# Taking 110 products of zeros out of the front of a gated-recurrence and gated-MLP kernel

## The chip, the cores and the metric

The kernel runs on one core of a Trainium2 chip. The metric is the time of one execution on the device in microseconds (us), measured from outside; the profile of one execution shows the span from that execution's first instruction to its last. TensorE (PE in the rows) multiplies, its weight loads are shown apart (PEld); VectorE (DVE), ScalarE (ACT) and GpSimd (POOL) do the rest, and SyncE (SP) issues nearly all DMA transfers.

## What is computed

For 4 batches and 8 heads, a recurrence over 768 tokens with a 48x48 state and a gate for each row, and then a gated MLP with a mixing matrix over the tokens:

```python
f = 1.0 / (1.0 + np.exp(-f_logit))
for t in range(S):
    state = f[:, :, t, :, None] * state + np.einsum('bhd,bhe->bhde', k[:, :, t], v[:, :, t])
    y[:, :, t] = np.einsum('bhd,bhde->bhe', q[:, :, t], state)
# x: y with the heads side by side, (4, 768, 384)
h = np.maximum(x @ w_in, 0.0)
u, v = (h[..., :d_ff // 2], h[..., d_ff // 2:])
v_n = (v - mean(v)) / np.sqrt(var(v) + 1e-06)
v_s = np.einsum('ts,bsd->btd', w_spatial, v_n) + b_spatial[None, :, None]
return ((u * v_s) @ w_out).astype(np.float32)
```

## The kernel before

The tokens of a batch are cut into 6 blocks of 128, which makes 24 blocks, numbered n = 0 to 23. The recurrence is done block by block in chunk form. For each block: `LF`, `LK`, `LQ` load the gate logits, keys and queries, and values; `c`, `e` clip the logits and take a logarithm of the gate (ACT, lines 325 and 326); `z` sums these along the tokens, for blocks 0 to 7 by products with a triangle on TensorE (line 336); `h` and `g` are exponentials of the sums (ACT, 342 and 347); `q` and `k` scale queries and keys (DVE, 357 and 353); `X` makes the scores (PE, 381); `w` and `m` take them out of PSUM (ACT 387, DVE 391); `YS`, `kv` and `Yq` are the products with values and state (PE, 435, 405, 447); `r0`, `r1`, `r2` update the state (DVE 411/413 and 419, POOL 426); `ys`, `xt`, `xh`, `xl` take the block's output out, transpose it (PE, 459) and split it into two parts for the MLP.

The MLP works on these outputs with every operand split into a rounded part and a rest, in three passes: `V` (PE, 492), `U` (PE, 577), `S` (PE, 591) and `O` (PE, 622), with their steps on the other engines. Before `V` can run, its weights have to be loaded (`LV`, `LU`, `LO`, line 242, from the 64-bit form in which they lie in memory) and converted: `ca` (ACT, 251), `ct` (DVE, 256 to 258), `ch` (ACT, 265) and `cl` (DVE, 271). The token matrix is split by `wh` (ACT, 289) and `wl` (DVE, 293) after its loads `LW`.

The order of all steps is written out in one table, `PLAN`. A loop runs through it, and each step issues its instructions, so the table gives the order on every engine; an engine takes its own instructions strictly in that order, and waits by semaphores are put in from the data. Nothing moves a step at run time.

One kind of step, `D:n`, computes nothing that is used: n products of a tile of zeros, `junk`, with itself, into a PSUM tile `warm` that `W0` takes at the start and `W1` gives back after block 4's `r1`. They stand in the table between the steps of blocks 0 to 4:

```python
    def step_W0():
        mm.take("warm")

    def step_D(count):
        for _ in range(count):
            nc.tensor.matmul(mm.of("warm")[:, 0:2 * P], junk[:, 0:P], junk[:, 0:2 * P], start=True, stop=True)

    def step_W1():
        mm.done("warm")
```

`junk` is set to zero on DVE (line 206) ahead of everything else, and is written later by ACT (line 526), which only wants a sum and throws the elements away.

Of the kernel before, what the change touches and what calls it, by code (L numbers as in the profile page):

```python
# [41 lines left out]


PLAN = """
    LF:1 LF:0 constants W0 LF:2 LQ:1 LQ:0 c:1 e:1 LK:1 c:0 c:2 e:0 D:23 z:1 LK:0 e:2 D:1 z:0 LV:1 h:1 D:1 z:2 g:1
# [4 lines left out]
    z:4 xl:1 fm:3 ca:O,1 LQ:4 r0:2 c:5 r1:2 LW:2,0 D:1 V:0,1 ca:U,0 ct:O,1 ca:U,1 e:5 X:3 Yq:2 vr:0,1 LF:6 z:5 r2:2  # L50
    m:3 LK:6 w:3 ct:U,0 ys:2 D:1 YS:3 h:4 D:1 xt:2 g:4 kv:3 xh:2 LQ:5 wh:2,0 r0:3 c:6 r1:3 D:8 Yq:3 ch:U,0 xl:2 r2:3
    D:3 V:0,2 ys:3 k:4 h:5 q:4 g:5 cl:U,0 e:6 X:4 k:5 vr:0,2 xt:3 LK:7 z:6 m:4 fm:4 fm:5 xh:3 nm:0,0 w:4 xl:3 YS:4
    LF:7 vc:0,2 wl:2,0 D:1 U:0,0,1 sq:0,2 q:5 vc:0,0 ct:U,1 U:0,0,0 sq:0,0 vc:0,1 kv:4 sq:0,1 X:5 LQ:6 r0:4 c:7
    ur:0,0,0 r1:4 W1 Yq:4 LF:8 na:0,0 w:5 m:5 r2:4 V:0,3 nb:0,0 h:6 nc:0,0 g:6 fm:6 q:6 vh:0,2 YS:5 k:6 kv:5 ys:4
    vl:0,2 X:6 e:7 LQ:7 c:8 xt:4 LF:9 m:6 vr:0,3 z:7 r0:5 e:8 bs:0,3 Yq:5 r1:5 w:6 z:8 YS:6 h:7 kv:6 ys:5 q:7 g:7
    LQ:8 xt:5 r0:6 fm:7 vh:0,0 r1:6 Yq:6 k:7 xh:5 vl:0,0 xh:4 X:7 ch:U,1 xl:5 r2:6 LF:10 xl:4 w:7 V:0,5 cl:U,1 moe
    h:8 g:8 m:7 fm:8 vh:0,1 LB q:8 V:0,4 vr:0,5 vl:0,1 ys:6 bs:0,5 ch:O,1 xt:6 k:8 vr:0,4 YS:7 kv:7 xh:6 bs:0,4 X:8
    ur:0,0,1 LQ:9 xl:6 U:0,0,3 w:8 LF:11 cl:O,1 na:0,1 m:8 V:1,0 nb:0,1 ur:0,0,3 nc:0,1 LW:0,1 vn:0,5 U:0,0,2 vn:0,3
    vh:0,5 vn:0,4 vh:0,3 vl:0,5 vh:0,4 vl:0,3 vr:1,0 ur:0,0,2 vl:0,4 wh:0,1 bs:1,0 S:0,0,3 c:11 c:9 e:11 c:10 wl:0,1
    e:9 S:0,0,0 LO:0 r0:7 sg:0,0,3 e:10 z:9 z:10 Yq:7 YS:8 r1:7 sm:0,0,3 ys:7 sg:0,0,0 kv:8 ca:O,0 xt:7 z:11 LQ:10  # L60
    S:0,0,1 sh:0,0,3 xh:7 sl:0,0,3 xl:7 sm:0,0,0 ct:O,0 sh:0,0,0 U:0,1,0 V:1,1 ur:0,1,0 sl:0,0,0 ch:O,0 r2:7
    sg:0,0,1 cl:O,0 h:9 U:0,1,1 vr:1,1 LW:1,1 q:9 g:9 r0:8 sm:0,0,1 S:0,0,2 ur:0,1,1 r1:8 bs:1,1 r2:8 sh:0,0,1 k:9
    h:10 g:10 sl:0,0,1 fm:9 wh:1,1 Yq:8 k:10 X:9 ys:8 q:10 U:0,1,3 wl:1,1 w:9 LF:12 m:9 fm:10 xt:8 ur:0,1,3 sg:0,0,2
    X:10 LW:2,1 xh:8 sm:0,0,2 YS:9 xl:8 w:10 kv:9 LF:13 m:10 sh:0,0,2 V:1,2 sl:0,0,2 c:12 r0:9 e:12 LQ:11 r1:9
    O:0,0,0 r2:9 vr:1,2 z:12 h:11 U:1,0,2 g:11 bs:1,2 fm:11 oc:0,0,0 na:1,0 wh:2,1 od:0,0,0 c:13 O:0,0,2 k:11 nb:1,0
    wl:2,1 ur:1,0,2 e:13 nc:1,0 S:0,1,0 vn:1,0 oc:0,0,2 vn:1,2 od:0,0,2 vn:1,1 z:13 O:0,0,1 sg:0,1,0 sm:0,1,0
    S:0,1,2 oc:0,0,1 sh:0,1,0 od:0,0,1 sl:0,1,0 U:1,0,0 sg:0,1,2 S:0,1,3 ur:1,0,0 Yq:9 sg:0,1,3 YS:10 ys:9 q:11
    kv:10 xt:9 sm:0,1,3 r0:10 LQ:12 X:11 xh:9 r1:10 sh:0,1,3 Yq:10 LF:14 w:11 S:0,1,1 sl:0,1,3 ys:10 m:11 h:12 xl:9
    g:12 fm:12 q:12 k:12 xt:10 vh:1,0 sg:0,1,1 YS:11 vh:1,2 c:14 kv:11 vh:1,1 X:12 vl:1,0 LQ:13 e:14 U:0,1,2 r0:11
    sm:0,1,1 LF:15 m:12 r1:11 vl:1,2 h:13 Yq:11 w:12 z:14 V:1,3 ur:0,1,2 ys:11 q:13 g:13 vl:1,1 xh:10 xt:11 sh:0,1,1  # L70
    k:13 YS:12 vr:1,3 sl:0,1,1 kv:12 xh:11 X:13 xl:10 fm:13 LQ:14 sm:0,1,2 r0:12 U:1,0,1 w:13 LF:16 bs:1,3 sh:0,1,2
    r1:12 V:1,4 ur:1,0,1 m:13 h:14 xl:11 g:14 fm:14 c:15 V:1,5 sl:0,1,2 e:15 c:16 k:14 vr:1,4 z:15 U:1,1,0 e:16
    bs:1,4 vr:1,5 O:0,1,2 ur:1,1,0 z:16 bs:1,5 Yq:12 oc:0,1,2 YS:13 na:1,1 ys:12 od:0,1,2 kv:13 q:14 nb:1,1 O:0,1,0
    LQ:15 r0:13 nc:1,1 vn:1,4 vn:1,5 vh:1,4 xt:12 X:14 vn:1,3 oc:0,1,0 vl:1,4 xh:12 od:0,1,0 Yq:13 vh:1,3 O:0,1,1
# [36 lines left out]

# [712 lines left out]
```

## Time and profile before

| | |
|---|---|
| median of 3 runs | 361.62 us (361.6 to 361.71) |
| the profiled execution | 361.57 us, of which the span is 359.9 us |
| PE busy | 348.2 us (97% of the span), 4688 products |
| DVE busy | 217.1 us (60%) |
| ACT busy | 177.2 us (49%) |
| POOL busy | 64.1 us (18%) |
| granted TensorE clock, mean | 0.997 |

The share of a busy engine says little about what a stretch is worth; the front, up to some 50 us, has loads, weight conversions and short products that wait for each other, and behind it the long products of the MLP fill PE. In the rows an fp32 product stands as two records, so a step `X` with 16 products is a row of x32.

### The profile page before, as it was taken

The numbers are of one execution on the slowest core, as the hardware profiler recorded it, in microseconds if no ns is written. First come the engines' busy times: TensorE is split into PE (matmuls) and PEld (weight loads), VectorE is DVE, ScalarE is ACT, GpSimd is POOL, SyncE is SP. The second block draws the span as 40 slices with busy tenths as digits, with TensorE's granted clock in tenths as the row PEclk, the third lists the DMA queues.
The fourth block names the chain that finished last, engine by engine and source line by source line (L and its number), as shares of the span: only waits on it lengthen the run. The fifth ranks groups of instructions, "written<-read, shape, count | busy, mean of one in ns | idle before, by whom it ended". The sixth has DMA issues, their size and how long they took to land.

```text
span 359.9 us, 10676 instructions
## 1 busy us (share of the span) xinstructions
PE 348.2 (97%) x4688; PEld 319.2 (89%) x4688; DVE 217.1 (60%) x417; ACT 177.2 (49%) x355; POOL 64.1 (18%) x82
## 2 busy tenths in 40 slices
PE   7999999999999999999999999899999999999993
...
PEclk9999999999999999999999999999999999999998
...
GB/s 258 326 323 292 97 169 165 244 102 67 136 151 25 105 120 111 128 50 0 111 117 85 104 155 53 156 47 22 2 0 2 24 46 25 44 0 2 9 59 75
DMA packets 14983, 36.03 MB, mean 100 GB/s; under 512 B 1488, under 2 KB 10192, under 8 KB 14928
## 3 DMA queue, kind: packets, MB, share of 16 engines
...
q10 hardware_dynamic: 144, 0.20, 0.2%
...
## 4 chain that ended last, share of the span: by engine, by line
PE 84%; DVE 7%; DMA 4%; ACT 2%; issue 1%; SPq 0%; DVEq 0%; ACTq 0%
PE mm L591 27%; PE mm L622 13%; PE mm L577 13%; PE mm L492 12%; PE bp L381 5%; PE bp L447 3%; DMA late<-w_cv 3%; PE mm L672 2%; PE bp L435 2%; PE mm L459 2%; PE mm L336 2%; DMA fkq<-fkq 2%; PE bp L405 2%; DVE q L357 1%; DVE fkq L331 1%
## 5 line engine op out<-in xcount | busy, mean ns | idle before, releaser
L607 POOL TENSOR_TENSOR uT<-gt,uT 128x384 f32<-128x384 f32 x32 | 35.9, 1122 | 159.5 <-DVE gt L600 102.2
L615 DVE TENSOR_TENSOR gl<-uT,gh 128x384 fp32r<-128x384 f32 x32 | 18.6, 585 | 35.3 <-ACT gh L611 25.2
L591 PE MATMUL mm<-w_sph,vnh 128*128 128x384 f32 x192 | 39.7, 341 | 0.0
L591 PE MATMUL mm<-w_spl,vnh 128*128 128x384 f32 x192 | 39.0, 338 | 0.0
L591 PE MATMUL mm<-w_sph,vnl 128*128 128x384 f32 x192 | 39.0, 338 | 0.0
L600 DVE TENSOR_TENSOR gt<-mm,b_bc 128x384 f32<-128x384 f32 x32 | 17.8, 555 | 34.9 <-PE mm L591 34.7
L611 ACT CAST gh<-uT 128x384 fp32r<-128x384 f32 x32 | 16.4, 514 | 42.0 <-POOL uT L607 35.1
L582 ACT ACTIVATE uT<-mm 128x384 f32<-128x384 f32 x32 | 15.7, 490 | 41.1 <-PE mm L577 41.1
L591 PEld LDWEIGHTS mm<-w_sph,vnh 128*128 128x128 f32 x192 | 33.8, 188 | 0.7 <-ACT vnh L558 0.3
L591 PEld LDWEIGHTS mm<-w_spl,vnh 128*128 128x128 f32 x192 | 34.2, 188 | 0.0
L591 PEld LDWEIGHTS mm<-w_sph,vnl 128*128 128x128 f32 x192 | 34.2, 188 | 0.0
L366 POOL COPY ends<-F 112x4 f32<-112x4 f32 x24 | 10.9, 453 | 98.0 <-ACT F L342 98.0
L357 DVE TENSOR_TENSOR q<-fkq,F 112x512 f32<-112x512 f32 x24 | 19.6, 816 | 9.5 <-PE bp L447 5.4
L381 PE MATMUL bp<-q,fkq 48*64 48x112 f32 x768 | 23.6, 261 | 0.7 <-DVE q L357 0.7
L577 PE MATMUL mm<-xTh,w_inh 128*128 128x384 f32 x96 | 23.5, 353 | 0.0
L381 PEld LDWEIGHTS bp<-q,fkq 48*64 48x64 f32 x768 | 18.8, 133 | 4.0 <-issue 1.6
L512 DVE BATCH_NORM_STATS2 six<-vr 128x6 f32<-128x512 f32 x21 | 14.4, 686 | 12.9 <-ACT vr L506 12.9
L391 DVE TENSOR_TENSOR sc<-bp,mask 128x512 f32<-128x512 f32 x24 | 16.5, 689 | 9.3 <-ACT W L387 3.7
L577 PE MATMUL mm<-xTh,w_inl 128*128 128x384 f32 x96 | 22.1, 338 | 0.0
L577 PE MATMUL mm<-xTl,w_inh 128*128 128x384 f32 x96 | 22.1, 338 | 0.0
L622 PE MATMUL mm<-w_outh,gh 128*128 128x384 f32 x96 | 21.9, 344 | 0.0
L492 PE MATMUL mm<-w_inh,xTh 128*128 128x512 f32 x72 | 21.7, 409 | 0.0
...
## 6 DMA issues: line engine op xcount, KB each, us to landing
...
```

What stands on the lines that cost most here:

```text
L357: other("q", n, nc.vector).tensor_tensor(qs[n % 2][:, :, :, 0:C], *(x.rearrange("p (j c t) -> p j c t", c=T // C, t=C) for x in (parts(n)[ ...
L381: nc.tensor.matmul(sc[to, e, cs], k[dr, at:at + C], qs[n % 2][dr, j, chunk], start=True, stop=True)
L391: nc.vector.tensor_tensor(Ss[n % 2].rearrange("p (e j t) -> p e j t", e=2, t=C), scores(n)[:, :, :, 0:C], mask.unsqueeze(1).unsqueeze(1).b ...
L492: nc.tensor.matmul(acc, xs[:, c, ut * P:(ut + 1) * P], ws[:, c, G:FF], start=i == 0, stop=i == 3 * KX - 1)
L577: nc.tensor.matmul(acc[:, 0:TH], ws[:, kx, cs], xs[:, kx, :], start=i == 0, stop=i == 3 * KX - 1)
L582: nc.scalar.activation(uTs.take((b, th, c)), mm.of(("u", b, th, c))[:, 0:TH], AF.Relu)
L591: nc.tensor.matmul(acc[:, 0:TH], vns.of((b, ks))[va][:, cs], w_sp_s[wb][:, ks, th * TH:(th + 1) * TH], start=i == 0, stop=i == 3 * KS - 1,)
L600: nc.vector.tensor_tensor(gts.take((b, th, c)), mm.of(("s", b, th, c))[:, 0:TH], b_bc[:, th * TH:(th + 1) * TH], op=ALU.add)
L607: nc.gpsimd.tensor_tensor(uT, gts.of((b, th, c)), uT, op=ALU.mult)
L611: nc.scalar.copy(gs.take((b, th, c), HU)[0], uTs.of((b, th, c)))
L615: nc.vector.tensor_tensor(lo, uTs.of((b, th, c)), hi.bitcast(F32), op=ALU.subtract)
L622: nc.tensor.matmul(acc[:, 0:DM], gs.of((b, th, c))[ga][:, ts], w_out_s[wb][:, c, :], start=c == cs[0] == 0 and ga == wb == 0, stop=c == cs ...
```

## The change

Every `D` step is taken out of `PLAN`: D:23, 1, 1, 8, 4, 7, 14, 1, 5, 22, 9, 1, 1, 1, 8, 3 and 1, together 110 products and their 110 weight loads. The order of all other steps, the tiles, `W0` and `W1` (so the PSUM tile stays taken as long as before) and the setting of `junk` stay. The table is set in lines of the same width again and is one line shorter, so each line number after it is smaller by one. The first line of the table, before and after:

```diff
-    LF:1 LF:0 constants W0 LF:2 LQ:1 LQ:0 c:1 e:1 LK:1 c:0 c:2 e:0 D:23 z:1 LK:0 e:2 D:1 z:0 LV:1 h:1 D:1 z:2 g:1
+    LF:1 LF:0 constants W0 LF:2 LQ:1 LQ:0 c:1 e:1 LK:1 c:0 c:2 e:0 z:1 LK:0 e:2 z:0 LV:1 h:1 z:2 g:1 q:1 h:0 k:1
```

On PE, at the scores of the first two blocks (`X:1` writes bp_134, `X:0` writes bp_135, L381 before and L380 after), the order before is:

```order
L381 MATMUL bp_134<-q_124,fkq_113 64x112 x16
L672 LDWEIGHTS junk
L672 MATMUL mm_130<-junk 128x256
L672 LDWEIGHTS junk
L672 MATMUL mm_130<-junk 128x256
L672 LDWEIGHTS junk
L672 MATMUL mm_130<-junk 128x256
L672 LDWEIGHTS junk
L672 MATMUL mm_130<-junk 128x256
L381 MATMUL bp_135<-q_123,fkq_112 64x112 x16
```

and of the change, with `YS:0`, `kv:0` and `Yq:0` behind it:

```order
L380 MATMUL bp_134<-q_124,fkq_113 64x112 x16
L380 MATMUL bp_135<-q_123,fkq_112 64x112 x16
L434 MATMUL bp_134<-val_115,sc_117 64x48 x16
L404 MATMUL bp_134<-val_115,W_119 48x48 x16
L446 MATMUL bp_134<-sB_127,q_123 64x48 x8
```

The D:4 between the two scores is gone, and so are D:7 and D:14, which stood before `YS:0` and before `Yq:0`.

On PE, around block 3's `YS:3`, `xt:2` and `kv:3` (L435, L459 and L405), where PE has little idle time, the order before is:

```order
L336 MATMUL mm_131<-tri,fkq_114 48x128
L672 LDWEIGHTS junk
L672 MATMUL mm_130<-junk 128x256
L435 MATMUL bp_134<-val_116,sc_118 64x48 x16
L672 LDWEIGHTS junk
L672 MATMUL mm_130<-junk 128x256
L459 MATMUL mm_133<-ident,ysb 128x128 x3
L405 MATMUL bp_134<-val_116,W_120 48x48 x16
```

and of the change, with the first row of `Yq:3` behind it:

```order
L335 MATMUL mm_131<-tri,fkq_114 48x128
L434 MATMUL bp_134<-val_116,sc_118 64x48 x16
L458 MATMUL mm_133<-ident,ysb 128x128 x3
L404 MATMUL bp_134<-val_116,W_120 48x48 x16
L446 MATMUL bp_134<-sA_126,q_124 64x48 x2
```

Two single products are gone, and the D:8 between `kv:3` and `Yq:3`.

On PE, at the end of `Yq:3` (L447) and at `V:0,2` (L492), from where PE has work without a break, the order before is:

```order
L447 MATMUL bp_134<-sB_128,q_124 64x48 x2
L672 LDWEIGHTS junk
L672 MATMUL mm_130<-junk 128x256
L672 LDWEIGHTS junk
L672 MATMUL mm_130<-junk 128x256
L672 LDWEIGHTS junk
L672 MATMUL mm_130<-junk 128x256
L492 MATMUL mm_132<-w_inh,xTh_136 128x512 x3
L492 MATMUL mm_132<-w_inl,xTh_136 128x512 x3
L492 MATMUL mm_132<-w_inh,xTl_137 128x512 x3
```

and of the change:

```order
L446 MATMUL bp_134<-sB_128,q_124 64x48 x2
L491 MATMUL mm_132<-w_inh,xTh_136 128x512 x3
L491 MATMUL mm_132<-w_inl,xTh_136 128x512 x3
L491 MATMUL mm_132<-w_inh,xTl_137 128x512 x3
L380 MATMUL bp_135<-q_123,fkq_113 64x112 x16
```

The D:3 is gone. On DVE, ACT, POOL and SP the order is the same before and after.

## Rows read from the trace of the kernel before

**Rows 1.** The page's table of the span in 40 equal slices of 9 us: busy tenths of PE, and the granted TensorE clock in tenths.

```profile
PE   7999999999999999999999999899999999999993
PEclk9999999999999999999999999999999999999998
```

**Rows 2.** The chain of work that ended last, its pieces in order of time up to 50 us: start us, us, engine, tile, line.

```profile
2.11 4.75 PE mm L672 x23
6.86 1.02 PE mm L336 x15
7.88 0.21 PE mm L672
...
10.35 0.98 PE mm L672 x8
11.33 0.93 PE bp L381 x32
12.25 0.54 PE mm L672 x4
12.80 0.97 PE bp L381 x32
13.79 0.69 DVE sc L391
...
17.32 0.36 DVE sA L419
...
21.68 9.63 DMA late<-w_cv
...
36.00 0.21 PE mm L672
...
36.82 0.21 PE mm L672
...
37.87 0.98 PE mm L672 x8
...
38.93 0.68 PE bp L447 x32
39.62 0.43 PE mm L672 x3
40.05 2.10 PE mm L492 x9
...
45.18 0.22 PE mm L672
```

**Rows 3.** The products of line 672, by line over the first 46 us (count, busy us, mean ns), then those that start from 3.8 to 4.9 us and those that start from 6.1 us on (min/median/max ns); last, the step `z:1` of line 336.

```profile
L672 PE MATMUL mm<-junk 128*128 128x256 bf16 x110 | 17.0, 301 | 2.1 <-DVE rescale L214 2.1
L672 PE MATMUL mm<-junk x6: 421/421/422, 3.8 to 4.9; 128*128 128x256 bf16 x6
L672 PE MATMUL mm<-junk x91: 270/273/397, 6.1 to 45.1; 128*128 128x256 bf16 x91
L336 PE MATMUL mm<-tri,fkq x16: 272/273/323, 6.8 to 7.6; 128*64 128x128 f32 x8, 128*48 128x128 f32 x8
```

**Rows 4.** The timeline of the other engines in the front: start us, us, engine, line, operation, out<-in, count, and in brackets the idle time ahead of it and what ended it.

```profile
4.75 0.52 ACT L326 ACTIVATE fkq<-fkq 128x384 f32<-128x384 f32 x1
9.17 0.60 ACT L342 ACTIVATE F<-mm 112x512 f32<-112x512 f32 x1
10.41 0.68 DVE L353 SCALAR_TENSOR_TENSOR fkq<-fkq 112x512 f32<-112x512 f32 x1
16.05 2.44 POOL L321 TENSOR_SCALAR fkq<-fkq 128x384 f32<-128x384 f32 x1 [5.52 <-DVE words L257]
19.29 0.33 SPq L317 DMA_DIRECT2D val<-vv  x1
19.66 0.95 SPq L283 DMA_DIRECT2D spat<-w_spT  x2
23.10 0.83 ACT L289 CAST w_sph<-spat 128x768 fp32r<-128x768 f32 x1 [1.84 <-DMA spat<-w_spT]
38.70 0.55 DVE L474 TENSOR_TENSOR xTl<-mm,xTh 128x384 fp32r<-128x384 f32 x1
```

**Rows 5.** The timeline of PE where three longer groups of zero products stand, and the step behind each (columns as in rows 4; the last two rows are `X:2` and the first pass of `V:0,0`).

```profile
15.56 1.73 PE L672 MATMUL mm<-junk 128*128 128x256 bf16 x14
17.73 0.49 PE L447 MATMUL bp<-sB,q 48*64 48x48 f32 x10 [0.44 <-DVE sA L419]
...
21.26 2.58 PE L672 MATMUL mm<-junk 128*128 128x256 bf16 x22
...
24.38 1.16 PE L672 MATMUL mm<-junk 128*128 128x256 bf16 x9
...
25.81 1.00 PE L381 MATMUL bp<-q,fkq 48*64 48x112 f32 x32
26.74 0.97 PE L492 MATMUL mm<-w_inh,xTh 128*128 128x512 f32 x3
```

**Rows 6.** The last 6 us by stretch: length, busy us of PE, PEld, DVE, ACT, POOL (instructions in brackets), granted clock, DMA share, GB/s.

```profile
354.00:356.00 2.00, 0.01 (x1) 0.00 (x0) 0.36 (x1) 0.36 (x2) 0.00 (x0) 1.00 0.71 253
356.00:358.00 2.00, 0.00 (x0) 0.00 (x0) 0.00 (x0) 0.00 (x0) 0.00 (x0) 0.99 0.21 67
358.00:360.00 2.00, 0.00 (x0) 0.00 (x0) 0.00 (x0) 0.00 (x0) 0.00 (x0) 0.50 0.03 8
```

More of the change, by code (lines that the diff above doesn't have):

```diff
@@ L50 @@
[L50 to L74, printed above, removed]
@@ new lines @@
+    LF:4 ch:V,1 r1:0 Yq:0 YS:1 LK:3 ys:0 kv:1 ct:V,0 e:3 xt:0 LQ:3 xh:0 LW:1,0 z:3 cl:V,1 ch:V,0 LW:0,0 cl:V,0 LU:1
+    r2:0 xl:0 wh:1,0 c:4 r0:1 h:2 r1:1 Yq:1 LU:0 g:2 q:2 ys:1 k:2 e:4 xt:1 wl:1,0 X:2 LO:1 wh:0,0 fm:2 V:0,0 r2:1
+    m:2 w:2 wl:0,0 h:3 g:3 LF:5 q:3 YS:2 LK:5 xh:1 k:3 kv:2 vr:0,0 z:4 xl:1 fm:3 ca:O,1 LQ:4 r0:2 c:5 r1:2 LW:2,0
+    V:0,1 ca:U,0 ct:O,1 ca:U,1 e:5 X:3 Yq:2 vr:0,1 LF:6 z:5 r2:2 m:3 LK:6 w:3 ct:U,0 ys:2 YS:3 h:4 xt:2 g:4 kv:3
+    xh:2 LQ:5 wh:2,0 r0:3 c:6 r1:3 Yq:3 ch:U,0 xl:2 r2:3 V:0,2 ys:3 k:4 h:5 q:4 g:5 cl:U,0 e:6 X:4 k:5 vr:0,2 xt:3
@@ new lines @@
+    LK:7 z:6 m:4 fm:4 fm:5 xh:3 nm:0,0 w:4 xl:3 YS:4 LF:7 vc:0,2 wl:2,0 U:0,0,1 sq:0,2 q:5 vc:0,0 ct:U,1 U:0,0,0
+    sq:0,0 vc:0,1 kv:4 sq:0,1 X:5 LQ:6 r0:4 c:7 ur:0,0,0 r1:4 W1 Yq:4 LF:8 na:0,0 w:5 m:5 r2:4 V:0,3 nb:0,0 h:6
+    nc:0,0 g:6 fm:6 q:6 vh:0,2 YS:5 k:6 kv:5 ys:4 vl:0,2 X:6 e:7 LQ:7 c:8 xt:4 LF:9 m:6 vr:0,3 z:7 r0:5 e:8 bs:0,3
+    Yq:5 r1:5 w:6 z:8 YS:6 h:7 kv:6 ys:5 q:7 g:7 LQ:8 xt:5 r0:6 fm:7 vh:0,0 r1:6 Yq:6 k:7 xh:5 vl:0,0 xh:4 X:7
+    ch:U,1 xl:5 r2:6 LF:10 xl:4 w:7 V:0,5 cl:U,1 moe h:8 g:8 m:7 fm:8 vh:0,1 LB q:8 V:0,4 vr:0,5 vl:0,1 ys:6 bs:0,5
@@ new lines @@
+    ch:O,1 xt:6 k:8 vr:0,4 YS:7 kv:7 xh:6 bs:0,4 X:8 ur:0,0,1 LQ:9 xl:6 U:0,0,3 w:8 LF:11 cl:O,1 na:0,1 m:8 V:1,0
+    nb:0,1 ur:0,0,3 nc:0,1 LW:0,1 vn:0,5 U:0,0,2 vn:0,3 vh:0,5 vn:0,4 vh:0,3 vl:0,5 vh:0,4 vl:0,3 vr:1,0 ur:0,0,2
+    vl:0,4 wh:0,1 bs:1,0 S:0,0,3 c:11 c:9 e:11 c:10 wl:0,1 e:9 S:0,0,0 LO:0 r0:7 sg:0,0,3 e:10 z:9 z:10 Yq:7 YS:8
+    r1:7 sm:0,0,3 ys:7 sg:0,0,0 kv:8 ca:O,0 xt:7 z:11 LQ:10 S:0,0,1 sh:0,0,3 xh:7 sl:0,0,3 xl:7 sm:0,0,0 ct:O,0
+    sh:0,0,0 U:0,1,0 V:1,1 ur:0,1,0 sl:0,0,0 ch:O,0 r2:7 sg:0,0,1 cl:O,0 h:9 U:0,1,1 vr:1,1 LW:1,1 q:9 g:9 r0:8
@@ new lines @@
+    sm:0,0,1 S:0,0,2 ur:0,1,1 r1:8 bs:1,1 r2:8 sh:0,0,1 k:9 h:10 g:10 sl:0,0,1 fm:9 wh:1,1 Yq:8 k:10 X:9 ys:8 q:10
+    U:0,1,3 wl:1,1 w:9 LF:12 m:9 fm:10 xt:8 ur:0,1,3 sg:0,0,2 X:10 LW:2,1 xh:8 sm:0,0,2 YS:9 xl:8 w:10 kv:9 LF:13
+    m:10 sh:0,0,2 V:1,2 sl:0,0,2 c:12 r0:9 e:12 LQ:11 r1:9 O:0,0,0 r2:9 vr:1,2 z:12 h:11 U:1,0,2 g:11 bs:1,2 fm:11
+    oc:0,0,0 na:1,0 wh:2,1 od:0,0,0 c:13 O:0,0,2 k:11 nb:1,0 wl:2,1 ur:1,0,2 e:13 nc:1,0 S:0,1,0 vn:1,0 oc:0,0,2
+    vn:1,2 od:0,0,2 vn:1,1 z:13 O:0,0,1 sg:0,1,0 sm:0,1,0 S:0,1,2 oc:0,0,1 sh:0,1,0 od:0,0,1 sl:0,1,0 U:1,0,0
@@ new lines @@
+    sg:0,1,2 S:0,1,3 ur:1,0,0 Yq:9 sg:0,1,3 YS:10 ys:9 q:11 kv:10 xt:9 sm:0,1,3 r0:10 LQ:12 X:11 xh:9 r1:10 sh:0,1,3
+    Yq:10 LF:14 w:11 S:0,1,1 sl:0,1,3 ys:10 m:11 h:12 xl:9 g:12 fm:12 q:12 k:12 xt:10 vh:1,0 sg:0,1,1 YS:11 vh:1,2
+    c:14 kv:11 vh:1,1 X:12 vl:1,0 LQ:13 e:14 U:0,1,2 r0:11 sm:0,1,1 LF:15 m:12 r1:11 vl:1,2 h:13 Yq:11 w:12 z:14
+    V:1,3 ur:0,1,2 ys:11 q:13 g:13 vl:1,1 xh:10 xt:11 sh:0,1,1 k:13 YS:12 vr:1,3 sl:0,1,1 kv:12 xh:11 X:13 xl:10
+    fm:13 LQ:14 sm:0,1,2 r0:12 U:1,0,1 w:13 LF:16 bs:1,3 sh:0,1,2 r1:12 V:1,4 ur:1,0,1 m:13 h:14 xl:11 g:14 fm:14
@@ new lines @@
+    c:15 V:1,5 sl:0,1,2 e:15 c:16 k:14 vr:1,4 z:15 U:1,1,0 e:16 bs:1,4 vr:1,5 O:0,1,2 ur:1,1,0 z:16 bs:1,5 Yq:12
+    oc:0,1,2 YS:13 na:1,1 ys:12 od:0,1,2 kv:13 q:14 nb:1,1 O:0,1,0 LQ:15 r0:13 nc:1,1 vn:1,4 vn:1,5 vh:1,4 xt:12
+    X:14 vn:1,3 oc:0,1,0 vl:1,4 xh:12 od:0,1,0 Yq:13 vh:1,3 O:0,1,1 LF:17 m:14 ys:13 vl:1,3 w:14 xl:12 vh:1,5 r1:13
+    xt:13 oc:0,1,1 V:2,0 xh:13 vl:1,5 od:0,1,1 h:15 xl:13 g:15 fm:15 q:15 S:1,0,3 vr:2,0 c:17 bs:2,0 e:17 k:15 z:17
+    S:1,0,0 sg:1,0,3 V:2,1 sg:1,0,0 sm:1,0,0 sh:1,0,0 S:1,0,1 vr:2,1 sl:1,0,0 bs:2,1 S:1,1,1 sg:1,0,1 sm:1,0,1
@@ new lines @@
+    sh:1,0,1 sl:1,0,1 U:1,1,1 sg:1,1,1 S:1,0,2 ur:1,1,1 sm:1,1,1 sh:1,1,1 sl:1,1,1 X:15 sg:1,0,2 YS:14 sm:1,0,2 m:15
+    w:15 LF:18 kv:14 S:1,1,2 sh:1,0,2 r0:14 r1:14 sl:1,0,2 h:16 LQ:16 g:16 fm:16 k:16 Yq:14 sg:1,1,2 YS:15 ys:14
+    c:18 kv:15 q:16 e:18 xt:14 LQ:17 U:1,0,3 r0:15 r1:15 xh:14 z:18 h:17 Yq:15 ur:1,0,3 X:16 ys:15 q:17 U:1,1,2 g:17
+    LF:19 xl:14 sm:1,0,3 w:16 m:16 fm:17 sh:1,0,3 xt:15 k:17 YS:16 ur:1,1,2 sl:1,0,3 kv:16 xh:15 U:2,0,1 sm:1,1,2
+    xl:15 LQ:18 r0:16 r1:16 O:1,0,0 c:19 ur:2,0,1 h:18 g:18 fm:18 e:19 O:1,0,2 k:18 oc:1,0,0 z:19 od:1,0,0 O:1,0,1
```

65 lines of the change are left out of this document (27 added, 38 removed).

## The prediction

> **What bounds the kernel now.** I read the page's table of the span first [rows 1]: PE is busy in nine tenths or more of nearly every slice, at full clock. The reader should not stop there, since up to 45 us a part of that busy time is products of zeros: 110 of them, 17.0 us busy [rows 3]; as their ends overlap with the next start, they hold PE for less. The chain of waits [rows 2] says which of them lie on the path that sets the end: 4.75 us at the start, then 0.21, 0.21 (its twin behind z:0), 0.98, 0.54, 0.21, 0.21, 0.98, 0.43 and 0.22, together 8.7 us. D:14, D:22 and D:9 [rows 5] are not on it; the chain runs over DVE and a weight load there. So 8.7 us is the most that can be had, and each piece is worth only what is left until the next late thing.
>
> Then the clock. The column of the granted clock is at its full value in the first slice too, but the products of zeros themselves say otherwise: 421 ns each from 3.8 to 4.9 us, 270 ns from about 6.1 us on [rows 3]. 23 of them take 4.75 us, a step of some 0.2 us, and 8 of them 0.98 us, a step of 0.12 us [rows 2]: 256 columns at 1.2 and at 2.4 GHz. So PE started at the low level and rose after some 4 us of products without a break, just ahead of z:1, whose products take 273 ns [rows 3]. Every real product of this run had the high level.
>
> **The change part by part**, with the clock rising once and staying.
>
> *Start.* z:1 began at 6.86 [rows 2], when D:23 was through; the logarithm it needs was ready at 4.75 + 0.52 = 5.27 [rows 4]. It can begin 1.5 us earlier, but now at the low level: a block of z, 1.02 us at the high level, is bounded by 1.0 (nothing about it slows) and 2.0 us (all of it goes by the clock). I take 1.9, near the upper end, since the products of zeros nearly doubled. z:1 ends at about 7.3 instead of 7.9, z:0 at about 9.1 (9.1 before). If the clock rises after as long a run as before, it does so near 9.5, and z:2 ends near 10.5, where D:8 begins at 10.35 now. So D:23 and the two single products give nothing up to here: +0.15.
>
> *D:8 and D:4.* X:1 began at 11.33 behind D:8 and begins near 10.5; its keys and queries come from z:1 and are earlier than before. X:0 began at 12.80 behind D:4. What is late next is k:0 on DVE, which ended at 10.41 + 0.68 = 11.09 [rows 4] and hangs on h:0 at 9.17, that is on z:0, which does not move. So X:0 follows X:1 without a wait, near 11.5, and ends near 12.4 instead of 13.77. m:0 began at 13.79 [rows 2]; m:1 and w:1, which take turns on the scores ahead of it, now push it to about 12.7. Gain at this place: 1.1 us.
>
> *D:7, D:14, D:5, D:22, D:9.* Behind m:0 the chain is DVE's, with the weight conversions up to sA at 17.32 to 17.68, for which Yq:0 waits at 17.73 [rows 5], and so is most of what follows; PE only fills in. These 57 products are worth 0: their cover is DVE. They cost nothing today either, except if the clock needs them (below). The 1.1 us is handed on: kv:1 ends 1.1 earlier, so LQ:3 (19.29) and the loads behind it in SP's queue, spat (19.66) and late (21.68) [rows 2, 4], go 1.1 earlier; h:2 stands behind the cast that waited 1.84 us for spat [rows 4]. One thing does not move: c:3 on POOL, 16.05 to 18.49 [rows 4], whose load follows k:0. e:3 and the cast of the weights behind it on ACT gain only some 0.4, but h:2 and X:2 do not hang on these. X:2 (25.81) [rows 5] comes about 0.9 earlier, V:0,0 with it.
>
> *Single products from 31 to 37 us.* Here PE goes from step to step; two on the chain at 0.21 each (36.00 and 36.82) and one at 31 us for perhaps half as much: 0.5. kv:3 is 1.4 earlier.
>
> *D:8 at 37.87.* It ends at 38.85 and Yq:3 begins at 38.93; Yq:3 waits for the state sum on DVE, which ran meanwhile. Worth 0.
>
> *D:3 at 39.62.* 0.43 on the path. Late next would be xl:2 on DVE, which ends at 38.70 + 0.55 = 39.25 [rows 4], ahead of Yq:3's end. Worth 0.43. *D:1 at 45.18:* 0.22.
>
> The sum is 0.9 + 0.5 + 0.43 + 0.22 = 2.05 us. Behind 45 us nothing is touched, and all loads there are issued by what PE, DVE and SP do, so what is early stays early. 361.57 - 2.05 = 359.5 us for the profiled execution, 0.05 below the median of the runs; I say 359.6. The bounds in this case: z at no slowing gives 1.5 us less at the start, of which X:0 keeps perhaps half (359.0); the 0.9 halved by small losses between DVE and POOL gives 360.2.
>
> **The rivals.** What the products of zeros may have bought is the clock, and it is the clock that decides.
>
> *Rival 1, it falls between and recovers.* Behind X:0 the new kernel has little for PE until X:2: Yq:0, YS:1 and kv:1 (some 1.5 us between 17.73 and 19.29 [rows 4, 5]), a transpose, z:3, Yq:1, and gaps without a product of about 2.1 and 2.4 us, where D:14 (1.73) and D:22 (2.58) stand now [rows 5]. If one group at 17 us and X:2 with the two short steps ahead of it run at half clock, kv:1 loses 1.3 and the loads go where they were; X:2's group, 1.9 us, loses up to 1.6. V:0,0 is then 0.6 late, and the 1.15 of later single pieces leaves -0.5: 361.1 us. For it: nothing in this trace has so loose a PE in the middle. Against it: the one fall here came with no product at all for about 4 us [rows 6], the last one ending at 354.0, and the new gaps are shorter. The Trainium skill ("TensorE: Matmul & The Clock Gate", section on the second HAM failure mode) says that short idle stretches between groups of products, if frequent, let the clock go to and fro between its two levels. By that rule this rival is what happens; no run here shows it yet.
>
> *Rival 2, slower: it stays low until the long products of V:0,0.* X:1 and X:0 take up to 0.95 more each, so m:0 is 0.7 late instead of 1.1 early; Yq:0, YS:1 and kv:1 add 1.3, so the loads, h:2 and X:2 start about 2.1 late; X:2 adds 0.95 and V:0,0 (2.1 us of products at the high level) up to 2.1 more. That is 5.1 at worst, 3.1 if V:0,0 runs at the high level, less the 1.15 of later pieces: +2.0 to +4.0, I take 364.6 us. It decides as soon as low clock costs more than 2.05 us on the path, which the two X and one more group do. For it: all work of 5 to 25 us is short products with waits between, and z is the only long run. Against it: z:1, z:0, z:2, X:1 and X:0 follow each other for 7 us, as long a run as the one which raised the clock here.
>
> *Rival 3, the clock rises only behind X:0, then stays.* m:0 is where it was or slightly late, and what remains is the 1.15 of later pieces, less 0.5: about 361.0 us.
>
> **How the numbers follow.** Clock up early and kept: 0.45. Rival 1: 0.20. Rival 2: 0.25. Rival 3: 0.10. A measurement of this kernel can tell about 0.2%, 0.72 us. Faster by more than that: all but a little of the first case, a quarter of rival 1 and a third of rival 3, 0.53. Slower: rival 2 and a trace of rival 1, 0.27. The same: 0.20. The time is the first case's, 359.6 us. The range goes from its lower bound, 359.0, to 364.0, which leaves out 0.03 below and about two thirds of rival 2 above, 0.17; the first case's own range is 359.0 to 360.3.
>
> **What would show it.** Right: z:1 begins near 5.3 us with products longer than 273 ns, the shorter duration comes before X:0, m:0 begins about 1.1 us earlier, the late load is issued about a microsecond earlier, V:0,2 begins near 38.0, and the distance to each later step is what it was. Wrong: a clock below 1 between 12 and 30 us, scores or V:0,0 at nearly double length, or the load of late issued after 21.7. The forecast fails if short products do not raise or hold the clock as the products of zeros did, and if c:3 or the first loads, which do not move, hold more than e:3.

## The result and the profile after

The changed kernel takes 364.77 us (median of 8 runs, 363.25 to 365.92) where the kernel before takes 361.93 us (8 runs, 361.05 to 363.7). The ratio is 1.0062, 95% interval 1.0042 to 1.0083: slower by some 2.2 us by the ratio (the medians are 2.84 us apart), where 359.6 us and a gain were forecast. The profiled execution is the shortest of the eight, 363.25 us with a span of 361.6 us, 1.7 us above the span before.

The page of after: busy time of the engines, and the two rows of the table of 40 slices that answer to [rows 1].

```profile
PE 339.7 (94%) x4578; PEld 313.9 (87%) x4578; DVE 216.6 (60%) x417; ACT 177.1 (49%) x355; POOL 62.1 (17%) x82
...
PE   4669898999999999999999999999999999999993
...
PEclk9958999999999999999999999999999999999997
```

PE is busy 8.5 us less and the kernel is longer. The clock's row has a 5 and an 8 in its third and fourth slice, 18 to 36 us, where [rows 1] shows full speed.

The same stretch of after in pieces of 2 us: length, busy us of PE, PEld, DVE, ACT and POOL (instructions), granted clock, DMA share, GB/s.

```profile
13.00:15.00 2.00, 1.04 (x64) 0.95 (x64) 1.90 (x3) 0.72 (x2) 0.00 (x0) 1.00 1.05 407
15.00:17.00 2.00, 0.20 (x4) 0.20 (x6) 1.93 (x5) 1.44 (x2) 0.00 (x0) 0.84 0.79 275
17.00:19.00 2.00, 2.00 (x76) 2.00 (x76) 1.86 (x3) 0.66 (x2) 1.67 (x1) 0.50 0.97 327
19.00:21.00 2.00, 1.75 (x25) 1.26 (x19) 2.00 (x2) 1.63 (x4) 1.96 (x3) 0.50 0.38 114
21.00:23.00 2.00, 1.43 (x14) 1.03 (x10) 1.56 (x4) 0.51 (x1) 0.00 (x0) 0.50 0.88 262
23.00:25.00 2.00, 1.10 (x32) 0.97 (x32) 0.59 (x2) 0.95 (x2) 0.00 (x0) 0.50 1.03 399
25.00:27.00 2.00, 0.71 (x3) 0.50 (x3) 1.59 (x3) 1.97 (x5) 1.56 (x2) 0.50 1.03 418
27.00:29.00 2.00, 2.00 (x34) 1.60 (x34) 0.61 (x2) 0.94 (x2) 0.95 (x1) 0.50 1.02 402
29.00:31.00 2.00, 2.00 (x7) 1.63 (x8) 1.82 (x3) 1.31 (x3) 0.27 (x1) 0.75 1.01 313
```

Behind `kv:0`, which ends at 14.7 us, PE has no product until `Yq:0` at 16.80. D:14 stood there, and D:7 ahead of `YS:0`, where PE is now idle for 0.86 us. A clock of 0.84 over 15 to 17 us means full speed for 1.36 us of it and half for the rest, so it fell near 16.4 us. It is at half until 30.0 us (0.75 over 29 to 31), although PE was busy without a break from 17 to 19 us, and it rises only while `X:2` and `V:0,0` follow each other.

What half the clock costs stands in the products by line: `z` (L335) and `X` (L380) of after, each at both levels (count, min/median/max ns, first and last start).

```profile
L335 PE MATMUL mm<-tri,fkq x10: 421/421/448, 5.4 to 6.3; 128*64 128x128 f32 x5, 128*48 128x128 f32 x5
...
L335 PE MATMUL mm<-tri,fkq x12: 272/273/397, 9.3 to 10.0; 128*64 128x128 f32 x6, 128*48 128x128 f32 x6
...
L380 PE MATMUL bp<-q,fkq x64: 256/256/307, 10.6 to 12.5; 48*64 48x112 f32 x64
...
L380 PE MATMUL bp<-q,fkq x32: 391/391/446, 27.1 to 28.5; 48*64 48x112 f32 x32
```

And the chain of waits of after up to 48 us (start us, us, what), which answers to [rows 2]:

```profile
10.56 1.04 PE bp L380 x32
...
11.81 1.04 PE bp L380 x32
...
12.87 0.69 DVE sc L390
...
16.39 0.37 DVE sA L418
...
18.73 0.70 PE bp L404 x26
...
19.82 4.21 DMA spat<-w_spT
...
24.79 0.59 ACT F L341
...
26.29 0.90 PE mm L458 x3
...
27.19 1.70 PE bp L380 x32
28.90 2.82 PE mm L491 x9
...
41.82 2.29 PE mm L491 x9
...
47.14 3.37 PE mm L576 x18
```

Read against the trace of before, the lead and the lag of each place are: `m:0` 0.92 us early (12.87 against 13.79), `sA` 0.93 early, then `LQ:3` 0.16 late (issued at 19.45 against 19.29 [rows 4]), `h:2` 0.95 late (24.79 against 23.84; it stands behind the cast that waits for `spat`), `X:2` 1.3 late, the start of `V:0,0` 2.1 and its end 2.6 late, `V:0,2` 1.8, `U` at 47 us 1.74, the span 1.7. Between 16.4 and 31.7 us the kernel loses some 3.5 us. Of these 1.1 lie in `Yq:0`, `YS:1` and `kv:1`, 0.4 in `xt:1` (0.90 us), 0.77 in `X:2` (1.70 against 0.93) and 0.54 in `V:0,0` (2.82 against 2.28), together 2.8 at half clock; 0.8 is the load `spat`, which landed 4.21 us behind its issue instead of 3.4 [rows 4]. The gain at the start (0.93) and behind 31 us (0.85) don't pay for that.

### The profile page after: what moved, and what is told of

Its sections match the earlier page's. It is cut to its first block, busy times and chain, and to the rows that moved or that the text cites. A ratio compares the mean times of both kernels' runs of the same rounds, so it can differ in the third digit from the quotient of the medians.

```text
span 361.6 us, 10455 instructions
## 1 busy us (share of the span) xinstructions
PE 339.7 (94%) x4578; PEld 313.9 (87%) x4578; DVE 216.6 (60%) x417; ACT 177.1 (49%) x355; POOL 62.1 (17%) x82
## 4 chain that ended last, share of the span: by engine, by line
PE 84%; DMA 6%; DVE 5%; ACT 1%; issue 1%; SPq 1%; DVEq 0%; ACTq 0%
PE mm L590 26%; PE mm L491 14%; PE mm L576 13%; PE mm L621 13%; PE bp L380 6%; PE bp L446 3%; DMA fkq<-fkq 3%; PE bp L434 3%; PE mm L458 2%; PE bp L404 2%; DMA late<-w_spT 2%; DMA spat<-w_spT 1%; DVE fkq L330 1%; PE mm L335 1%; DVE q L356 1%
## 5 line engine op out<-in xcount | busy, mean ns | idle before, releaser
L365 POOL COPY ends<-F 112x4 f32<-112x4 f32 x24 | 9.7, 402 | 100.8 <-ACT F L341 100.8
L356 DVE TENSOR_TENSOR q<-fkq,F 112x512 f32<-112x512 f32 x24 | 18.7, 780 | 11.7 <-PE bp L446 5.8
L380 PE MATMUL bp<-q,fkq 48*64 48x112 f32 x768 | 24.4, 266 | 0.9 <-DVE fkq L352 0.6
L576 PE MATMUL mm<-xTh,w_inh 128*128 128x384 f32 x96 | 23.5, 353 | 0.0
L380 PEld LDWEIGHTS bp<-q,fkq 48*64 48x64 f32 x768 | 19.5, 136 | 4.3 <-issue 1.9
```

What stands on the lines that cost most here:

```text
L356: other("q", n, nc.vector).tensor_tensor(qs[n % 2][:, :, :, 0:C], *(x.rearrange("p (j c t) -> p j c t", c=T // C, t=C) for x in (parts(n)[ ...
L380: nc.tensor.matmul(sc[to, e, cs], k[dr, at:at + C], qs[n % 2][dr, j, chunk], start=True, stop=True)
L576: nc.tensor.matmul(acc[:, 0:TH], ws[:, kx, cs], xs[:, kx, :], start=i == 0, stop=i == 3 * KX - 1)
```

## The experiments

Each kernel was compared with runs of the kernel before on the same chip. Nothing that the output needs is left out anywhere. The products of zeros ("zero products" from here on) are counted as start (23, 1, 1, 8, 4), middle (7, 14, 1, 5, 22, 9) and late (1, 1, 1, 8, 3, 1).

**Which part costs.** `mid_only` and, once more, `mid_again` put the middle's 58 back into the changed kernel (pieces of the table's lines, as in all diffs below):

```diff
-    ct:V,1 LF:3 YS:0 kv:0
+    ct:V,1 LF:3 D:7 YS:0 kv:0
...
-    ch:V,1 r1:0 Yq:0 YS:1 LK:3 ys:0 kv:1 ct:V,0 e:3 xt:0
+    ch:V,1 r1:0 D:14 Yq:0 YS:1 LK:3 ys:0 kv:1 ct:V,0 e:3 D:1 xt:0
...
-    z:3 cl:V,1
+    D:5 z:3 cl:V,1
...
-    r1:1 Yq:1 LU:0 g:2 q:2 ys:1 k:2 e:4 xt:1
+    r1:1 D:22 Yq:1 LU:0 g:2 q:2 ys:1 k:2 e:4 D:9 xt:1
```

> Only the zero products between X:0 and X:2 are kept (D:7, 14, 1, 5, 22 and 9, 58 of the 110); those at the start and those behind 30 us are gone. Theory A (the loss of the change is the clock, which fell at 16.4 us when PE had little to do, and nothing else): the clock rises near 9.5 us as in the changed kernel and stays up to the end, m:0 begins near 12.9 us, V:0,2 near 38.0 to 38.5, and the time is 1.5 to 2.0 us below the kernel before, ratio 0.995 to 0.996. Rival B (the loss comes from the start: the sums z at the low clock and the loads that follow): slower than before by 1 us or more, ratio above 1.003. Rival C (the zero products are worth nothing either way and the loss is a chance of how DVE, POOL and the loads meet): within 0.2% of either side.

> The kernel that keeps the zero products between X:0 and X:2 alone, a second time, on the same chip as the next two. Theory L: 0.999 to 1.003 again, since what the start gains is taken by the loads of keys and of spat. The prediction's sum, had only the clock failed in it: 0.994 to 0.996.

Measured: 1.0012 (0.999 to 1.0033) and 0.9983 (0.9962 to 1.0005): no loss, but not the gain of theory A either (0.995 to 0.996). The clock holds, as the stretches of mid_again show (columns as above):

```profile
13.00:17.00 4.00, 3.59 (x89) 2.81 (x85) 3.81 (x8) 2.15 (x4) 0.26 (x1) 1.00 0.95 351
17.00:21.00 4.00, 3.93 (x108) 3.36 (x109) 3.86 (x5) 3.10 (x6) 3.85 (x3) 1.00 0.75 229
21.00:25.00 4.00, 3.95 (x62) 3.12 (x60) 2.03 (x5) 1.43 (x3) 0.04 (x1) 1.00 0.87 290
```

`no_mid` is the reverse: only the middle is taken out of the kernel before. `no_start` takes out only the start, `no_late` only the late ones:

```diff
-    e:0 D:23 z:1 LK:0 e:2 D:1 z:0 LV:1 h:1 D:1 z:2
+    e:0 z:1 LK:0 e:2 z:0 LV:1 h:1 z:2
...
-    q:0 D:8 X:1 k:0 LV:0 w:1 m:1 fm:1 D:4 X:0
+    q:0 X:1 k:0 LV:0 w:1 m:1 fm:1 X:0
```

> The zero products between X:0 and X:2 are gone (D:7, 14, 1, 5, 22 and 9), those at the start and behind 30 us are kept. Theory A: the clock falls between 16 and 18 us and comes back near 30 us, X:2 and V:0,0 run at the low level, and as the start is not earlier and the later zero products still stand on the path this is the slowest of the four: 3 to 5 us over the kernel before, ratio 1.008 to 1.014. Rival B: as fast as the kernel before, ratio 0.998 to 1.002. Rival C: 1.000 within 0.2%.

> The zero products ahead of X:0 are gone (D:23, 1, 1, 8 and 4), all later ones are kept. Theory A: clock up near 9.5 us and kept; m:0 near 12.9 us instead of 13.8, and the 0.9 us is handed on to the end: ratio 0.997 to 0.998. Rival B: as slow as the changed kernel or nearly so, ratio above 1.003. Rival C: 1.000 within 0.2%.

> The zero products behind X:2 are gone (six places from 31 us on, 15 products), all earlier ones are kept. Theory A: the clock stays up and PE is earlier by the pieces that stand on the path, 1.0 to 1.2 us by the prediction's terms: ratio 0.997. Rival C: 1.000 within 0.2%, since a wait for DVE is behind each piece.

Measured: no_mid 1.0093 (1.006 to 1.0125), no_start 1.0002 (0.9979 to 1.0025), no_late 1.0003 (0.9976 to 1.0029). So no_mid lost as theory A said, and the gains that it expected of the two others (0.997 to 0.998 and 0.997) did not come. The clock of no_mid falls near 16.4 us, is back in 24 to 26 us and at half again in 28 to 30:

```profile
16.00:18.00 2.00, 0.38 (x8) 0.38 (x9) 1.97 (x4) 1.70 (x2) 0.78 (x1) 0.60 0.78 234
...
24.00:26.00 2.00, 0.68 (x32) 0.59 (x32) 0.81 (x3) 1.80 (x4) 0.41 (x1) 1.00 1.05 403
28.00:30.00 2.00, 2.00 (x23) 1.53 (x16) 1.04 (x2) 0.40 (x2) 0.10 (x1) 0.50 1.04 412
```

So the loss comes with the 58 products of the middle, and it goes with the clock. The other half of the finding is that the 52 others, with the clock held, give nothing that can be measured. Without the middle they may give a little: no_mid, which keeps them, is 0.3% above the changed kernel, at intervals that overlap.

**How much of the middle the clock needs.** `gap_one` keeps only D:7 and D:14 of all 110, `gap_two` only the D:1, 5, 22 and 9 behind them, `half` half of each group (3, 7, 0, 2, 11, 4). Gap_one against the changed kernel:

```diff
-    LF:3 YS:0 kv:0
+    LF:3 D:7 YS:0 kv:0
...
-    r1:0 Yq:0
+    r1:0 D:14 Yq:0
```

> Of all zero products only D:7 and D:14 are kept, the 21 between X:0 and Yq:0 (13.5 to 17 us); none in the second loose stretch (19 to 26 us). Theory A1 (each loose stretch alone lowers the clock): the clock holds past 17 us, falls between 19 and 24 us, so X:2 and V:0,0 run at the low level until near 30 us; time 1.0 to 2.5 us over the kernel before, ratio 1.003 to 1.007. Rival A2 (only the first, emptiest stretch lowers it): clock at full value from 9.5 us to the end, time as with all zero products of the middle kept, ratio 0.999 to 1.003.

> Of all zero products only D:1, D:5, D:22 and D:9 are kept, the 37 between kv:1 and X:2 (19 to 26 us); none ahead of that. Theory A1: the clock falls near 16 us, the 37 products then run at some 0.2 us each, D:22 alone 4.7 us, so Yq:1 is late by about 1 us, but they bring the clock back between 23 and 27 us, ahead of V:0,0; time 0.5 to 2.0 us over the kernel before, ratio 1.0015 to 1.0055. Rival A2 (a long low clock costs little by itself, and what cost time was PE's order): 0.999 to 1.001.

> The zero products between X:0 and X:2 at half their number (3, 7, 0, 2, 11 and 4 instead of 7, 14, 1, 5, 22 and 9), no others. Theory A1: PE works about three quarters of these stretches, and the clock either holds throughout (then as with all of the middle, 0.999 to 1.003) or falls once; I expect that it holds. If it falls it costs as in the changed kernel, 1.004 to 1.008. Rival (the clock wants a PE without any break): it falls near 16 us.

Measured: 1.0061 (1.0035 to 1.0087), 1.007 (1.0038 to 1.0101) and 1.0052 (1.0021 to 1.0084). Gap_one, then gap_two, by stretch:

```profile
21.00:23.00 2.00, 0.00 (x0) 0.00 (x0) 1.94 (x5) 0.12 (x1) 0.00 (x0) 1.00 0.96 349
23.00:25.00 2.00, 0.68 (x32) 0.59 (x32) 0.74 (x2) 1.86 (x4) 0.47 (x1) 0.92 0.91 283
25.00:27.00 2.00, 1.62 (x19) 1.30 (x23) 1.66 (x3) 1.97 (x4) 2.00 (x2) 0.50 1.00 372
```

```profile
15.00:17.00 2.00, 0.15 (x15) 0.03 (x4) 1.93 (x4) 1.00 (x2) 0.22 (x1) 0.93 0.90 331
17.00:19.00 2.00, 1.74 (x54) 1.75 (x56) 1.86 (x4) 1.22 (x3) 2.00 (x2) 0.50 0.91 284
...
27.00:29.00 2.00, 2.00 (x44) 1.73 (x41) 1.12 (x2) 1.97 (x4) 1.49 (x1) 1.00 1.02 404
```

With the first gap filled the clock falls in the second, near 24.7 us; with the second filled it falls in the first, near 16.7. Either kernel loses nearly what the changed one loses, but not in the same way. In gap_one `X:2` and `V:0,0` run at half clock. In gap_two the clock is back at full near 23.5 us and these two have it; there the group ahead and `z:3` ran at half, and the zero products that are kept stand on the chain themselves, for 5.0 us of it between 19.84 and 27.93 us (its profiled execution is the slowest of its seven, 367.2 us). Half of the products is worse than all, 1.0052, where the clock was expected to hold: with the two longest of half's twelve executions left out (367.52 and 368.16 us, at 0.982 and 0.977), four had a mean granted clock of 0.990 or less and took 364.5 us on average, six had 0.994 or more and took 362.8 us. Even the profiled one of the six (363.39 us) shows half clock from about 26.1 to 29.5 us. So neither stretch can go bare, and half of each group is too little; how much less than the whole would do was not tried.

**Where the forecast gain went.** `early_keys` is mid_only with the loads of the first two blocks' keys issued earlier, since `q:1` waited for `LK:1` in mid_only:

```diff
-    W0 LF:2 LQ:1 LQ:0 c:1 e:1 LK:1 c:0 c:2 e:0 z:1 LK:0 e:2
+    W0 LK:1 LF:2 LK:0 LQ:1 LQ:0 c:1 e:1 c:0 c:2 e:0 z:1 e:2
```

> All zero products between X:0 and X:2 kept, none at the start or behind 30 us, and the loads of keys and queries of blocks 1 and 0 issued earlier in SP's queue: LK:1 ahead of LF:2, LK:0 ahead of the two loads of values. Theory L (with the start's zero products gone, the landing of LK:1 is what is late next; it came at 9.1 to 9.9 us in three kernels without them): q:1 waits for ACT's F and not for the load, X:1 begins near 10.4 us instead of 11.4, m:0 near 12.8 instead of 13.7, and the end comes 0.5 to 0.9 us earlier than with the middle alone kept; ratio to the kernel before 0.997 to 0.999. Rival (another load or the conversions on DVE are late next): X:1 earlier, ct:V,1 not, ratio 1.000 to 1.003.

Measured: 1.0046 (1.0015 to 1.0077), no gain, and above what the rival allowed too. The load that was now late is the gate logits of a first block, 5.58 us on the chain; `X:1` began at 11.13 us (11.37 in mid_only). Moving one load ahead here delayed another; the DMA share was 0.80 to 1.09 in the pieces of 2 us from 2 to 10 us.

`before_again` is the kernel before once more, unchanged, for the spread of its own steps:

> The kernel before, unchanged, profiled a second time. Theory L (the first profile had early loads: LK:1 landed 4.9 us and spat 3.4 us after their issue, in the profiles since 5.2 to 6.8 and 3.5 to 4.9): here LK:1 lands later than 8.5 us and spat 4 us or more after its issue, X:2 begins at 26.3 us or later instead of 25.81, with nothing changed. Rival (the early loads belong to the kernel with its zero products): X:2 within 0.3 us of 25.81. Time ratio 0.998 to 1.002 in either case.

Measured: 0.9992 (0.9969 to 1.0016). Its timeline at the cast that waits for the token matrix and at `X:2`, to be laid beside [rows 4, 5] (columns as there):

```profile
23.39 0.83 ACT L289 CAST w_sph<-spat 128x768 fp32r<-128x768 f32 x1 [2.43 <-DMA spat<-w_spT]
...
26.11 1.00 PE L381 MATMUL bp<-q,fkq 48*64 48x112 f32 x32
```

And mid_again, with the start's zero products gone:

```profile
23.57 0.83 ACT L289 CAST w_sph<-spat 128x768 fp32r<-128x768 f32 x1 [2.87 <-DMA spat<-w_spT]
26.29 1.00 PE L381 MATMUL bp<-q,fkq 48*64 48x112 f32 x32
```

The cast waits longer than in before_again, and `X:2` is not earlier. For before_again the expectation was half met: `q:1` began at 9.30 us, but `spat` landed 3.76 us behind its issue (4 or more expected) and `X:2` came at 26.11 us (26.3 or later expected, and 0.3 us from the 25.81 before, the edge of the rival's). `spat` landed 3.4 to 3.8 us behind its issue in three of the four traces that keep the start's zero products and issue it at the old place (4.3 in no_late), and 4.2 to 4.9 us in the eight that don't keep them. So it isn't shown whether the early landing of the first trace was chance or belongs to those products.

A second load matters. The chain of before doesn't run through `X:2`; behind the weight conversions on DVE it goes over a cast of weights and SP's queue to `late` at 21.68 us [rows 2], which lands at 31.31. The two rows of before's chain ahead of it:

```profile
20.43 0.84 ACT w_inh L265
...
21.27 0.36 SPq L242
```

In the chain of mid_again `late` stands too:

```profile
21.89 10.37 DMA late<-w_cv
```

`LQ:3` was issued 0.68 us earlier there than before (18.61 against 19.29), yet `late` was issued 0.21 later and landed 0.95 later, at 32.26; in no_start it was issued at 22.50 and landed at 32.15. So what the start gave was gone by the time these loads landed. `spat_early` takes the wait for `spat` out of the kernel before, with all 110 zero products kept, by issuing the load some 7.4 us earlier; `spat_early_2` is the same on another chip; `spat_early_mid` does it in mid_only, `spat_early_none` in the changed kernel, `spat_early_no_late` in the kernel without the late zero products:

```diff
-    LK:4 ca:V,0 LQ:2
+    LK:4 LW:1,0 ca:V,0 LQ:2
...
-    LQ:3 xh:0 LW:1,0
+    LQ:3 xh:0
```

> The kernel before with all its zero products; only the load LW:1,0 of spat is moved forward in SP's queue, from behind LQ:3 to behind LK:4 (from 19.7 to near 12.7 us). Theory L (the landing of spat, with the cast wh:1,0 and h:2 behind it on ACT, sets X:2): the cast begins near 21.3 us, right behind the cast of the weights, h:2 near 22.2, X:2 near 25.4, and the end comes 0.5 to 1.5 us earlier: ratio 0.996 to 0.999. Rival (X:2 hangs on Yq:1 and ys:1, or a later load is next): X:2 within 0.3 us of the kernel before or no gain at the end, 0.999 to 1.001.

> The same move of LW:1,0 in the kernel that keeps the zero products between X:0 and X:2 alone. Theory L: with that load out of the way the start's and the later pieces count: X:2 near 24.5 to 25.5 us, V:0,2 near 39, ratio to the kernel before 0.993 to 0.997, below both the kernel before and the changed one. Rival: 0.999 to 1.003, as without the move.

> The early load of the token matrix alone, a second time, as the base for the two others. Theory (the cast ahead of h:2 waits for that load): 0.9966 again, between 0.995 and 0.999, the cast of wh:1,0 begins near 20.8 us without a wait, V:0,2 near 39.4. Rival (the first ratio was a lucky draw): 1.000, V:0,2 near 39.9.

> The early load of the token matrix, and the 15 late zero products (31 to 45 us) taken out. Theory (the late pieces stand on the path, between V:0,1 and V:0,2, and were worth 0.9 us): V:0,1 to V:0,2 is 8.1 us instead of 8.75, V:0,2 near 38.7, and the ratio is 0.002 below that of spat_early_2. Rival (V:0,2 is reached by other things, and something behind it takes the rest): the ratio is that of spat_early_2 within 0.001. The clock stays at 0.99 or above under both.

> No zero products in the front, as in the changed kernel, and the load of the token matrix issued early. Theory (the change's loss is the clock alone, and the load only adds to it): the granted clock is at half from some point between 15 and 18 us for 5 us or more; h:2 no longer waits for the load, so X:2 begins at 25.5 to 26.5 instead of 27.1, and the ratio is 1.002 to 1.005, some 0.003 better than the changed kernel, still slower than spat_early_2 by 0.005. Rival (with the loose stretch shortened, the clock holds): mean clock 0.99, ratio 0.994 to 0.997.

| kernel | zero products kept | ratio (95%) | median us |
|---|---|---|---|
| spat_early | all | 0.9966 (0.9946 to 0.9987) | 360.94 |
| spat_early_mid | middle | 0.9969 (0.9946 to 0.9993) | 361.34 |
| spat_early_2 | all | 0.9971 (0.9948 to 0.9994) | 360.92 |
| spat_early_no_late | start, middle | 0.9963 (0.9939 to 0.9988) | 360.46 |
| spat_early_none | none | 1.0026 (1.0001 to 1.0052) | 362.88 |

The timeline of spat_early, where the load, the cast and `X:2` stand:

```profile
12.23 0.42 SPq L283 DMA_DIRECT2D spat<-w_spT  x1
...
20.81 0.83 ACT L289 CAST w_sph<-spat 128x768 fp32r<-128x768 f32 x1
...
25.59 1.00 PE L381 MATMUL bp<-q,fkq 48*64 48x112 f32 x32
```

The cast has no wait left, and the kernel is faster than both kernels of this case on two chips. Three things follow. First, with all the zeros gone and the load early, the kernel is still 1.96 us above spat_early_2 on the same chip (362.88 against 360.92), and spat_early_mid, which differs from it by the middle alone, is at 0.9969 against its 1.0026: what remains is the clock. Its stretches:

```profile
17.00:19.00 2.00, 1.24 (x39) 1.18 (x37) 1.97 (x3) 1.43 (x3) 1.24 (x2) 0.50 1.02 376
...
21.00:23.00 2.00, 2.00 (x18) 1.57 (x16) 0.39 (x1) 1.63 (x3) 0.78 (x1) 0.50 0.35 102
23.00:25.00 2.00, 0.36 (x12) 0.19 (x13) 1.97 (x5) 1.30 (x3) 0.41 (x2) 0.99 0.86 244
25.00:27.00 2.00, 1.39 (x43) 1.00 (x43) 2.00 (x3) 1.36 (x4) 0.67 (x1) 0.87 1.02 407
27.00:29.00 2.00, 2.00 (x33) 1.63 (x28) 0.54 (x2) 0.79 (x2) 0.00 (x0) 0.50 1.02 413
```

It comes back near 23 us, and falls again after a stretch with 0.36 us of products in 2. Second, the load does not explain by itself why the start is worth nothing: with it out of the way, spat_early_mid is no faster than spat_early. Its chain shows what is late next:

```profile
17.37 1.18 POOL fkq L321
...
19.70 1.09 PE mm L336 x15
20.79 2.51 PE mm L672 x22
```

`c:3` on POOL ends at 18.54 us, where it ended before (18.49 [rows 4]); the logarithm behind it lets `z:3` begin at 19.70, 0.33 us earlier than in spat_early, and from there PE is the chain up to `X:2`, with D:22 and D:9 (1.09 us) on it. They are on the chain of spat_early too, with the same 2.51 and 1.09 us. So once `spat` is early, the zero products that hold the clock are not free: they stand between `z:3` and `X:2`. `X:2` is 0.33 us earlier (25.26 against 25.59), and PE then stopped for 0.71 us in `z:4`; that is one execution, and a gain of a few tenths is below what the times can tell. Third, the late zero products do lie on the path, for about 0.4 us. From `V:0,1` to `V:0,2` pass 8.53 to 8.75 us in the six traces that have them (before, before_again, no_start, no_mid, spat_early, spat_early_2) and 8.09 to 8.19 in ten that have not, but 8.76 in mid_again, which has none either: its `z:5` waited 0.66 us for the logarithm, which stands behind the conversion of `late` on ACT. In the time, spat_early_no_late is 0.0008 below spat_early_2, which is no difference at these intervals; its rival had said so.

## Why the prediction was wrong

**The step that failed** is the condition of the whole sum, "with the clock rising once and staying", by which the products behind X:0 were worth 0. The rise came much as forecast, by 9.3 us: `z` ran at 421 ns, then at 272 ns. The staying did not: the clock was at half from 16.4 to 30.0 us and cost 2.8 us. What happened has the mechanism of rival 1, a fall behind X:0, at a price near that of rival 2: V:0,0 was reached at half clock too, and what was lost up to there, 3.5 us with the load, exceeded the gains, 0.93 and 0.85. Rival 1 was set aside with the argument that the one fall in the trace of before came after some 4 us without a product [rows 6], and that the new gaps are shorter. In after the clock was at half 1.7 us behind the last product. One fall in one trace does not show that the clock holds over a shorter gap; and what ran before it was another thing: products without a break there, short ones with waits between here. The rule of the Trainium skill that the prediction set beside rival 1 ("TensorE: Matmul & The Clock Gate", section on the second HAM failure mode), by which frequent short idle stretches let the clock go between its levels, agrees with spat_early_none (0.50 in 21 to 23 us, 0.99 in 23 to 25, 0.50 in 27 to 29) and with no_mid; in after the clock fell once in the front and came back once. The forecast had set a chance of 0.20 on rival 1.

**Point by point.**

- *Start, D:8 and D:4:* right. z:1 began at 5.41 (5.3 forecast), X:1 at 10.56 (10.5), X:0 at 11.81 (11.5), m:0 was 0.92 early (1.1). That it is worth that at the end was wrong, even with the clock held (no_start 1.0002).
- *D:7, D:14, D:5, D:22, D:9 worth 0, "except if the clock needs them":* the exception was the case. They are not on the chain of before, and they buy 2.8 us of the profiled execution. With `spat` early, D:22 and D:9 are on the chain.
- *The 1.1 us handed on to kv:1, the loads and X:2 (0.9):* failed twice. At half clock kv:1 gave it all back (the 1.3 of rival 1 measured 1.1), and `late` was issued at 21.95 us, one of the signs of being wrong that the prediction named. And with the clock held, the loads did not come earlier with their issues: `spat` landed 4.2 to 4.9 us behind its issue where the sum kept the 3.4 of [rows 4], and `late`, on which the chain of before runs, landed later (32.26 in mid_again). The sum took `late` as a load behind others in SP's queue; in before it stood behind the cast of weights, for which the prediction itself had only 0.4 us. With `spat` out of the way `c:3`, which does not move, sets X:2 over z:3, as the last sentence of the prediction named it. The load of `LK:1` varies as well: `q:1` began at 8.56 us in the profile of before, at 9.30 in that of before_again, the same kernel; 8.56 is the earliest of the seven traces that keep the start's zero products (up to 9.59).
- *Single products 0.5, D:8 0, D:3 0.43:* 0.93 forecast, 0.85 in after, about 0.4 between V:0,1 and V:0,2 in most pairs of traces, none of it to be told in the times. What the forecast named for D:8 alone holds for the rest: without them the chain of after goes from X:3 over DVE (scores, weight conversions and state sums, 37.00 to 40.92 us) to Yq:3.
- *D:1 at 45 us 0.22:* worth nothing. From V:0,2 to V:0,3 pass 10.92 us before and 10.91 after.
- *The range*, 359.0 to 364.0, did not hold the median of 364.77 us: its upper end left out two thirds of rival 2, which forecast 364.6 us. That rival 2 has nearly the measured time is luck: it had the clock low from the start to the long products, and X:1 and X:0 ran at full clock.

What stays open: whether the start and the late pieces are worth a few tenths with the clock held. The interval of mid_again goes down to 0.9962, 1.4 us. The kernels that hold the clock do it with zero products that can set X:2 themselves, so none of them tests the forecast's sum with a clock that holds by itself.
